# Retention with its state on VectorE, scaled k on ScalarE, later loads of v and an early stretch of zero products

## The chip, the cores and the metric

The kernel runs on one core of one Trainium2 chip. The metric is the device time of one execution in microseconds (us); each run of a kernel gives one such time, and the median counts. Five engines work side by side, each in the order of its own queue, and wait for one another through semaphores: TensorE (PE; PEld is its weight load) multiplies matrices into PSUM, VectorE (DVE) and ScalarE (ACT) work element by element on SBUF and PSUM, GpSimd (POOL) sets up constants, SyncE (SP) issues the loads and stores. Times of a trace are counted from the first instruction; the span ends with the last.

## The reference

Three stages follow each other: a retention (attention with a decaying state, 2 x 8 heads, 768 positions of 64 channels), a feed-forward layer with mish, and one with elu (1536 tokens, 512 to 2048 and back). The feed-forward weights come as 64-bit floats, everything else as 32-bit.

```python
for b in range(nb):                       # blocks of 64 positions
    qb, kb, vb = (q[:, :, sl], k[:, :, sl], v[:, :, sl])
    intra = np.einsum('bhic,bhjc->bhij', qb, kb) * Dmask[None]
    intra = np.einsum('bhij,bhjd->bhid', intra, vb)
    inter = np.einsum('bhid,bhde->bhie', qb * lam_pow[None], kv_state)
    out[:, :, sl] = intra + inter
    kb_dec = kb * rev_pow[None]
    kv_state = lam_block[None, :, None, None] * kv_state + np.einsum('bhsd,bhse->bhde', kb_dec, vb)
...
h = x @ w_in;  g = h * np.tanh(softplus(h));  x = g @ w_out
h = x @ w_in2; g = np.where(h > 0, h, np.exp(h) - 1);  out = g @ w_out2
```

## The kernel before

**Retention** (`retention`, L125) goes through 12 chunks of 128 positions, the two batches in turn; a chunk holds all 8 heads. Iteration n of the loop at L305 writes: the loads of chunk n+3 (`load`), perhaps a load of feed-forward weights (`beside_load`, table `LOAD`), the transposes of k and q of chunk n+1 (`transposes`, L211, copied out of PSUM by ScalarE as kT and qT, L215), the scores of chunk n (`scores`, L240), their product with the decay (`decay`, am, L247, VectorE), k and q of chunk n+1 scaled by powers of lam (`scaled`, kd at L223 and q2 at L230, both VectorE), and the outputs of chunk n-1 (`outputs`): the products o (L269) of the state with q2 and of v with am; xh, ScalarE's rounded copy of o (L274); the new state st (L289), which for a chunk with a state before it is eight products of the diagonal matrix dg (lam to the power 128) with the old state sbd and eight of kd with v, summed in PSUM; ScalarE's copy of st to sbd in two halves (L295), which the outputs of the batch's next chunk read; and xl, the rest o - xh, on VectorE (L296). The outputs' PSUM tile o has one buffer, so the next chunk's outputs wait for xh and xl.

**The weights.** A feed-forward weight tile is loaded as raw 64-bit words by SyncE (`w_load`) into one of four buffers and turned by eight VectorE steps and one ScalarE copy (`w_steps`, L94 to L118) into a high and a low 32-bit half. During retention `beside_step` puts one such step at a time between the retention's own VectorE instructions, from iteration 4 on; the steps of later tiles are spread over the feed-forward units by the tables `FIRST`, `SECOND` and `LATER`.

**Feed-forward.** A unit "in" is 12 products of 128x512 into h (three for each of four blocks of 128 channels: high by high, high by low, low by high), then the activation; a unit "out" is 12 products into y, added to acc on VectorE (L405).

**What sets the order.** A scheduler arranges the instructions of each engine by its own estimate; those given to `pin` keep the order in which they are written. Pinned are the loads, TensorE's retention products, the VectorE operations of the retention and the steps beside them. ScalarE's copies and the feed-forward products are not.

Of the kernel before, what the change touches and what calls it, by code (L numbers as in the profile page):

```python
# [8 lines left out]
F32 = mybir.dt.float32  # L9
# [9 lines left out]
def kernel(  # L19
# [12 lines left out]
    nc = tc.nc  # L32
# [53 lines left out]
    def w_steps(n):  # L86
# [27 lines left out]
        w_load(n + AHEAD)  # L114
# [10 lines left out]
    def retention(beside_load, beside_step, at_end):  # L125
# [12 lines left out]
        def pin(ins):  # L138
            tc.keep_in_program_order(ins)

        def load(n, parts=1):
            if n >= NC:
                return
            b, c = chunks[n]
            for nm, src in (("k", k), ("q", q), ("v", v)):
                t = io.tile([P, H, D], F32, tag=nm + "n", name=nm + "n")
                np_ = 1 if nm == "v" else parts
                for y in range(np_):
                    hs = slice(y * H // np_, (y + 1) * H // np_)
                    pin(nc.sync.dma_start(  # L150
                        out=t[:, hs],
                        in_=src[b, hs, c * P:(c + 1) * P, :].rearrange("h p d -> p h d"),
                    ))
                nat[n, nm] = t

        lam_b = cst.tile([P, H, 1], F32, name="lam_b")
        load(0, 2)
        nc.scalar.dma_start(out=lam_b.rearrange("p h o -> p (h o)"), in_=lam.partition_broadcast(P))
        for n in (1, 2):
            load(n)  # L160
# [27 lines left out]
        while m < P:  # L188
# [5 lines left out]

        dg = cst.tile([P, PR, P], F32, name="dg")
        nc.vector.tensor_tensor(
            out=dg, in0=ident.unsqueeze(1).to_broadcast([P, PR, P]),
            in1=lq[:, :, P - 1:P].to_broadcast([P, PR, P]), op=ALU.mult,
        )
# [4 lines left out]
        def transposes(n):  # L204
            b, c = chunks[n]
            out = []
            for nm in ("k", "q"):
# [7 lines left out]
                nc.scalar.activation(out=t, in_=ps, func=AF.Copy)  # L215
                out.append(t)
            tr[n] = out
        def scaled(n):
            c = chunks[n][1]
            q2 = kd = None  # L220
            if c < NCH - 1:
                kd = wk.tile([P, H, D], F32, tag="kd", name="kd", bufs=3)
                pin(nc.vector.tensor_tensor(  # L223
                    out=kd, in0=nat[n, "k"], in1=dm[:, :, P - 1:P].to_broadcast([P, H, D]),
                    op=ALU.mult,
                ))
                beside_step(n - 1, pin)
# [6 lines left out]
        def scores(n):  # L234
            kT, qT = tr[n]
            ps = psS.tile([P, 2, PR, P], F32, tag="sc", name="sc")
            for r in range(PR):
                for hh in range(2):
                    rows = slice(hh * D, (hh + 1) * D)
                    pin(nc.tensor.matmul(  # L240
                        ps[:, hh, r], lhsT=kT[rows, r], rhs=qT[rows, r], start=True, stop=True
                    ))
            sc[n] = ps

# [7 lines left out]
        def outputs(n):  # L252
# [21 lines left out]
            nc.scalar.activation(out=xh[t][:, :, col:col + P], in_=o, func=AF.Copy)  # L274
            if c < NCH - 1:

                st = psO.tile([P, PR, D], F32, tag="st", name="st")
                terms = []
                if c > 0:
                    terms += [  # L280
                        (r, hh, dg[:, r, hh * D:(hh + 1) * D], sbd[b][:, r, hh * D:(hh + 1) * D])
                        for r in range(PR) for hh in range(2)
                    ]
                terms += [
                    (r, hh, kd[:, 2 * r + hh], vn[:, 2 * r + hh])
                    for r in range(PR) for hh in range(2)
                ]
                for x, (r, hh, lt, rt) in enumerate(terms):
                    pin(nc.tensor.matmul(  # L289
                        st[hh * D:(hh + 1) * D, r], lhsT=lt, rhs=rt,  # L290
                        start=x < 2, stop=x >= len(terms) - 2, skip_group_check=True,
                    ))
                for hh in range(2):
                    rows = slice(hh * D, (hh + 1) * D)
                    nc.scalar.activation(out=sbd[b][rows, :, rows], in_=st[rows], func=AF.Copy)  # L295
# [5 lines left out]
            ))  # L301

        transposes(0)
        scaled(0)
        for n in range(NC + 1):  # L305
            load(n + 3)
# [4 lines left out]
            elif n < NC:  # L311
                if n + 1 < NC:
                    transposes(n + 1)
                scores(n)
# [7 lines left out]
            beside_step(n, pin)  # L322
        at_end()
# [130 lines left out]
    LOAD = {1: 0, 2: 1, 4: 2, 5: 3}  # L454
# [11 lines left out]
    def beside_step(n, pin):  # L466
        if n >= 4:
# [55 lines left out]
```

## Time and profile before

| | us |
|---|---|
| median of 3 runs (595.68 to 596.53) | 595.98 |
| the profiled execution | 595.6 |
| its span, first to last instruction | 593.8 |

A row of the profile's list of groups names the line, the engine, the operation, output and input tiles, the shape, the count, the busy time and the mean length of one. The chain of waits goes back from the last instruction: at each step to what released it, or to the instruction ahead of it on its engine; read in order of time, each piece has a start, a length, an engine and a line. A timeline row has a start, the time from its first start to its last end, the instruction, how many were merged, and in brackets for how long the engine was idle ahead of it and what ended that. A product of 32-bit floats stands as two records (x16 are eight products); a transpose stands as one.

### The profile page before, as it was taken

Reading aid. Unit: us, or ns where it says so; the run is one execution under the profiler, and the core shown is the slowest. Engines: PE = TensorE matmul, PEld = TensorE weight load, DVE = VectorE, ACT = ScalarE, POOL = GpSimd, SP = SyncE. Lnnn points to the kernel's source line nnn. Section 1 sums busy time; section 2 is a strip of 40 time slices with the busy share of each in tenths; the row PEclk is TensorE's granted clock in tenths of the full one; section 3 lists DMA queues with packets and bytes.
Section 4 is the critical chain, followed back from the end, with each engine's and each line's share of the span. In section 5 each row is a group of like instructions: output and inputs, shape, how many; then the busy total and the mean of one; then the engine's idle time right before and its main releaser. Section 6 shows DMA issues by size and latency. Waiting matters only on the chain.

```text
span 593.8 us, 8100 instructions
## 1 busy us (share of the span) xinstructions
PE 583.8 (98%) x3244; PEld 486.2 (82%) x3244; DVE 446.5 (75%) x822; ACT 217.2 (37%) x375; POOL 3.6 (1%) x10
## 2 busy tenths in 40 slices
PE   6999999999999999999999999999999999999997
PEld 4988888888888888888888888888888888888886
DVE  5798798999669943996489985999399966953342
ACT  3454445322242331341245453253254334244230
POOL 2000000000000000000000000000000000000000
PEclk9999999999999999999999999999999999999999
DMA  9999224224203220232013120233013210000112
GB/s 188 234 233 200 66 78 142 71 74 132 79 18 109 87 72 0 72 124 90 0 40 100 49 96 1 71 108 95 12 40 102 74 68 0 2 0 1 71 53 89
DMA packets 61029, 46.65 MB, mean 79 GB/s; under 512 B 38849, under 2 KB 55489, under 8 KB 60993
## 3 DMA queue, kind: packets, MB, share of 16 engines
q1 hardware_dynamic: 60848, 46.14, 27.6%
q8 instruction: 25, 0.41, 0.3%
q14 instruction: 12, 0.09, 0.0%
q10 hardware_dynamic: 144, 0.00, 0.0%
HBM read 43.00 MB, written 3.15 MB: 78 GB/s over the span
## 4 chain that ended last, share of the span: by engine, by line
PE 98%; DMA 1%; ACT 0%; issue 0%; DVE 0%; ACTq 0%
PE h L351 44%; PE y L393 44%; PE o L269 4%; PE sc L240 2%; PE st L289 1%; PE qTp L211 1%; PE kTp L211 1%; DMA kn<-in_k_dram 1%; ACT sbd L295 0%; ACT qT L215 0%; DVE acc L405 0%; ACTq L295 0%
## 5 line engine op out<-in xcount | busy, mean ns | idle before, releaser
L351 PE MATMUL h<-xh,w 128*128 128x512 f32 x768 | 241.2, 390 | 0.0
L351 PEld LDWEIGHTS h<-xh,w 128*128 128x128 f32 x768 | 143.9, 188 | 30.3 <-issue 0.3
L351 PE MATMUL h<-xl,w 128*128 128x512 f32 x384 | 149.4, 389 | 0.0
L393 PE MATMUL y<-g,w 128*128 128x512 f32 x576 | 133.0, 389 | 0.0
L393 PE MATMUL y<-w,g 128*128 128x512 f32 (+1 forms) x588 | 132.5, 385 | 0.0
L393 PEld LDWEIGHTS y<-w,g 128*128 128x128 f32 x588 | 108.9, 188 | 22.1
L393 PEld LDWEIGHTS y<-g,w 128*128 128x128 f32 x576 | 108.1, 188 | 22.5
L405 DVE TENSOR_TENSOR acc<-acc,y 128x512 f32<-128x512 f32 (+1 forms) x73 | 49.4, 677 | 57.7 <-PE y L393 57.6
L117 ACT ACTIVATE w<-m 128x512 fp32r<-128x512 f32 x64 | 40.2, 629 | 135.3 <-DVE m L115 71.9
L361 DVE TENSOR_TENSOR g<-g,g 128x512 fp32r<-128x512 f32 x96 | 65.7, 686 | 26.6 <-ACT g L360 26.3
L351 PEld LDWEIGHTS h<-xl,w 128*128 128x128 f32 x384 | 72.1, 188 | 15.0
L360 ACT ACTIVATE g<-g 128x512 fp32r<-128x512 f32 x96 | 59.8, 629 | 16.5 <-DVE g L378 15.4
L118 DVE TENSOR_TENSOR w<-m,w 128x512 fp32r<-128x512 f32 x64 | 43.7, 686 | 19.3 <-ACT w L117 18.6
L369 ACT ACTIVATE g<-h 128x512 f32<-128x512 f32 x48 | 28.1, 597 | 71.8 <-PE h L351 71.8
L375 ACT ACTIVATE e<-h 128x512 f32<-128x512 f32 x48 | 28.6, 596 | 65.7 <-PE h L351 65.0
L111 DVE SCALAR_TENSOR_TENSOR u<-raw,u 128x512 f32<-128x512 uint32 x64 | 43.6, 683 | 0.1
L104 DVE SCALAR_TENSOR_TENSOR b<-raw,b 128x512 int32<-128x512 int32 x64 | 43.6, 683 | 0.1
L115 DVE TENSOR_TENSOR m<-b,u 128x512 f32<-128x512 f32 x64 | 43.5, 683 | 0.1
L378 DVE SCALAR_TENSOR_TENSOR g<-e,h 128x512 f32<-128x512 f32 x48 | 32.7, 682 | 13.2 <-ACT e L376 13.2
L376 ACT ACTIVATE e<-e 128x512 f32<-128x512 f32 x48 | 30.2, 630 | 1.0
L107 DVE TENSOR_SCALAR u<-b 128x512 int32<-128x512 int32 x64 | 26.6, 420 | 0.3
L94 DVE TENSOR_SCALAR m<-raw 128x512 int32<-128x512 int32 x64 | 26.6, 420 | 0.3
(45 smaller groups left out, 288.2 us busy)
## 6 DMA issues: line engine op xcount, KB each, us to landing
raw<-in_moe_w_in_dram SPq DMA_DIRECT2D x32, 512.0 KB, 3.7
raw<-in_moe_w_out_dram SPq DMA_DIRECT2D x32, 512.0 KB, 3.3
vn<-in_v_dram SPq DMA_DIRECT2D x12, 256.0 KB, 5.1
kn<-in_k_dram SPq DMA_DIRECT2D x11, 256.0 KB, 5.1
qn<-in_q_dram SPq DMA_DIRECT2D x11, 256.0 KB, 5.2
out_dram<-acc SPq DMA_DIRECT2D x11, 256.0 KB, 2.0
kn<-in_k_dram SPq DMA_DIRECT2D x2, 128.0 KB, 3.3
qn<-in_q_dram SPq DMA_DIRECT2D x2, 128.0 KB, 3.4
```

The lines of the kernel that those rows point to most:

```text
L104: yield nc.vector.scalar_tensor_tensor(out=b, in0=hw, scalar=-0x40000000, in1=b, op0=ALU.bitwise_and, op1=ALU.bitwise_or)
L111: yield nc.vector.scalar_tensor_tensor(out=uf, in0=lw, scalar=2.0 ** -52, in1=uf, op0=ALU.mult, op1=ALU.mult)
L115: yield nc.vector.tensor_tensor(out=mf, in0=bf, in1=uf, op=ALU.add)
L117: nc.scalar.activation(out=w[:, 0], in_=mf, func=AF.Copy)
L118: yield nc.vector.tensor_tensor(out=w[:, 1], in0=mf, in1=w[:, 0].bitcast(F32), op=ALU.subtract)
L351: nc.tensor.matmul(h, lhsT=lt, rhs=rt, start=(kk == 0 and n == 0), stop=(kk == KD - 1 and n == 2),)
L360: nc.scalar.activation(out=gg[:, 0], in_=g, func=AF.Copy)
L361: nc.vector.tensor_tensor(out=gg[:, 1], in0=g, in1=gg[:, 0].bitcast(F32), op=ALU.subtract)
L376: nc.scalar.activation(out=e, in_=e, func=AF.Exp, scale=-1.0)
L378: nc.vector.scalar_tensor_tensor(out=g, in0=e, scalar=-1.0, in1=h, op0=ALU.add, op1=ALU.max)
L393: nc.tensor.matmul(y, lhsT=lt, rhs=rt, start=(i == 0 and n == 0), stop=(i == G - 1 and n == 2),)
L405: nc.vector.tensor_tensor(out=dst, in0=dst, in1=y, op=ALU.add)
```

## The change

- The state is kept in a tile sd for each batch. VectorE multiplies it by lam to the power 128 (after the products of st are issued) and, after xl and one weight step, adds st, which now holds kd and v alone; a batch's first state is copied. ScalarE copies sd, not st, to sbd. The eight products with dg and dg itself are gone.
- kd is made by ScalarE, eight pieces of 128x64, each scaled by a column of dm, in place of one VectorE multiplication.
- v of a chunk is loaded after k and q of the next one, and in the loop one iteration later than these.
- Eleven products of a tile of zeros are written at the beginning (`warm`): seven ahead of the transposes of chunk 0, four behind them.
- All of ScalarE's retention work is pinned. The weights' loads of tiles 4 to 7 are issued at iterations 9 to 12 and not by a step; the steps start at iteration 3 and stand at three places of an iteration, not four. The first two feed-forward units are issued after the last scores.

```diff
@@ -111,7 +111,8 @@
         yield nc.vector.scalar_tensor_tensor(
             out=uf, in0=lw, scalar=2.0 ** -52, in1=uf, op0=ALU.mult, op1=ALU.mult
         )
-        w_load(n + AHEAD)
+        if n >= PG - AHEAD:
+            w_load(n + AHEAD)
         yield nc.vector.tensor_tensor(out=mf, in0=bf, in1=uf, op=ALU.add)
         w = wp.tile([P, 2, DM], F32R, tag=f"w{side}", name=f"w{side}", bufs=(6, 8)[side])
         nc.scalar.activation(out=w[:, 0], in_=mf, func=AF.Copy)
@@ -137,16 +138,17 @@
 
         def pin(ins):
             tc.keep_in_program_order(ins)
-
-        def load(n, parts=1):
-            if n >= NC:
+            return ins
+
+        def load(n, names, parts=1):
+            if not 0 <= n < NC:
                 return
             b, c = chunks[n]
-            for nm, src in (("k", k), ("q", q), ("v", v)):
+            for nm in names:
+                src = {"k": k, "q": q, "v": v}[nm]
                 t = io.tile([P, H, D], F32, tag=nm + "n", name=nm + "n")
-                np_ = 1 if nm == "v" else parts
-                for y in range(np_):
-                    hs = slice(y * H // np_, (y + 1) * H // np_)
+                for y in range(parts):
+                    hs = slice(y * H // parts, (y + 1) * H // parts)
                     pin(nc.sync.dma_start(
                         out=t[:, hs],
                         in_=src[b, hs, c * P:(c + 1) * P, :].rearrange("h p d -> p h d"),
@@ -154,10 +156,11 @@
                 nat[n, nm] = t
 
         lam_b = cst.tile([P, H, 1], F32, name="lam_b")
-        load(0, 2)
+        load(0, "kq", 2)
         nc.scalar.dma_start(out=lam_b.rearrange("p h o -> p (h o)"), in_=lam.partition_broadcast(P))
         for n in (1, 2):
-            load(n)
+            load(n, "kq")
+            load(n - 1, "v")
 
         ident = cst.tile([P, P], F32, name="ident")
         make_identity(nc, ident)
@@ -191,12 +194,8 @@
                 in1=lq[:, :, m - 1:m].to_broadcast([P, PR, m]), op=ALU.mult,
             )
             m *= 2
-
-        dg = cst.tile([P, PR, P], F32, name="dg")
-        nc.vector.tensor_tensor(
-            out=dg, in0=ident.unsqueeze(1).to_broadcast([P, PR, P]),
-            in1=lq[:, :, P - 1:P].to_broadcast([P, PR, P]), op=ALU.mult,
-        )
+        lc = lq[:, :, P - 1:P].to_broadcast([P, PR, D])
+        sd = [cst.tile([P, PR, D], F32, name=f"sd{b}") for b in range(B)]
         sbd = [cst.tile([P, PR, P], F32, name=f"sbd{b}") for b in range(B)]
         for t in sbd:
             nc.gpsimd.memset(t, 0.0)
@@ -212,7 +211,7 @@
                         ps[:, r], x[:, 2 * r:2 * r + 2].rearrange("p h d -> p (h d)"), ident
                     ))
                 t = wk.tile([P, PR, P], F32, tag=nm + "T", name=nm + "T")
-                nc.scalar.activation(out=t, in_=ps, func=AF.Copy)
+                pin(nc.scalar.activation(out=t, in_=ps, func=AF.Copy))
                 out.append(t)
             tr[n] = out
         def scaled(n):
@@ -220,11 +219,11 @@
             q2 = kd = None
             if c < NCH - 1:
                 kd = wk.tile([P, H, D], F32, tag="kd", name="kd", bufs=3)
-                pin(nc.vector.tensor_tensor(
-                    out=kd, in0=nat[n, "k"], in1=dm[:, :, P - 1:P].to_broadcast([P, H, D]),
-                    op=ALU.mult,
-                ))
-                beside_step(n - 1, pin)
+                for x in range(H):
+                    pin(nc.scalar.activation(
+                        out=kd[:, x], in_=nat[n, "k"][:, x], func=AF.Copy,
+                        scale=dm[:, x, P - 1:P],
+                    ))
             if c > 0:
                 q2 = wk.tile([P, PR, P], F32, tag="q2", name="q2", bufs=3)
                 pin(nc.vector.tensor_tensor(out=q2, in0=tr[n][1], in1=lq, op=ALU.mult))
@@ -237,10 +236,11 @@
             for r in range(PR):
                 for hh in range(2):
                     rows = slice(hh * D, (hh + 1) * D)
-                    pin(nc.tensor.matmul(
+                    last = pin(nc.tensor.matmul(
                         ps[:, hh, r], lhsT=kT[rows, r], rhs=qT[rows, r], start=True, stop=True
                     ))
             sc[n] = ps
+            return last
 
         def decay(n):
             a = wk.tile([P, 2, PR, P], F32, tag="am", name="am")
@@ -271,39 +271,51 @@
                     start=x < 2, stop=x >= len(terms) - 2, skip_group_check=True,
                 ))
             t, col = divmod(n * P, TB)
-            nc.scalar.activation(out=xh[t][:, :, col:col + P], in_=o, func=AF.Copy)
+            pin(nc.scalar.activation(out=xh[t][:, :, col:col + P], in_=o, func=AF.Copy))
             if c < NCH - 1:
-
                 st = psO.tile([P, PR, D], F32, tag="st", name="st")
-                terms = []
+                for x in range(H):
+                    r, hh = divmod(x, 2)
+                    pin(nc.tensor.matmul(
+                        st[hh * D:(hh + 1) * D, r], lhsT=kd[:, x], rhs=vn[:, x],
+                        start=True, stop=True,
+                    ))
                 if c > 0:
-                    terms += [
-                        (r, hh, dg[:, r, hh * D:(hh + 1) * D], sbd[b][:, r, hh * D:(hh + 1) * D])
-                        for r in range(PR) for hh in range(2)
-                    ]
-                terms += [
-                    (r, hh, kd[:, 2 * r + hh], vn[:, 2 * r + hh])
-                    for r in range(PR) for hh in range(2)
-                ]
-                for x, (r, hh, lt, rt) in enumerate(terms):
-                    pin(nc.tensor.matmul(
-                        st[hh * D:(hh + 1) * D, r], lhsT=lt, rhs=rt,
-                        start=x < 2, stop=x >= len(terms) - 2, skip_group_check=True,
-                    ))
-                for hh in range(2):
-                    rows = slice(hh * D, (hh + 1) * D)
-                    nc.scalar.activation(out=sbd[b][rows, :, rows], in_=st[rows], func=AF.Copy)
+                    pin(nc.vector.tensor_tensor(out=sd[b], in0=sd[b], in1=lc, op=ALU.mult))
             pin(nc.vector.tensor_tensor(
                 out=xl[t][:, :, col:col + P],
                 in0=o,
                 in1=xh[t][:, :, col:col + P].bitcast(F32),
                 op=ALU.subtract,
             ))
-
+            beside_step(n + 1, pin)
+            if c < NCH - 1:
+                if c > 0:
+                    pin(nc.vector.tensor_tensor(out=sd[b], in0=sd[b], in1=st, op=ALU.add))
+                else:
+                    pin(nc.vector.tensor_copy(sd[b], st))
+                for hh in range(2):
+                    rows = slice(hh * D, (hh + 1) * D)
+                    pin(nc.scalar.activation(
+                        out=sbd[b][rows, :, rows], in_=sd[b][rows], func=AF.Copy
+                    ))
+
+
+        idle = cst.tile([P, P], F32, name="idle")
+        nc.vector.memset(idle, 0.0)
+
+        def warm(count):
+            ps = psO.tile([P, PR, P], F32, tag="o", name="warm")
+            for _ in range(count):
+                pin(nc.tensor.matmul(ps[:, 0], lhsT=idle, rhs=idle, start=True, stop=True))
+
+        warm(7)
         transposes(0)
+        warm(4)
         scaled(0)
         for n in range(NC + 1):
-            load(n + 3)
+            load(n + 3, "kq")
+            load(n + 2, "v")
             beside_load(n, pin)
             if n == 0:
                 scores(0)
@@ -311,7 +323,7 @@
             elif n < NC:
                 if n + 1 < NC:
                     transposes(n + 1)
-                scores(n)
+                last = scores(n)
             if n < NC:
                 decay(n)
             beside_step(n, pin)
@@ -319,8 +331,8 @@
                 scaled(n + 1)
             if n > 0:
                 outputs(n - 1)
-            beside_step(n, pin)
-        at_end()
+        with tc.issue_after(last.ins):
+            at_end()
         es.close()
 
 
@@ -451,7 +463,7 @@
         g, i = divmod(n, PG)
         u = (FIRST, SECOND)[g][i] if g < 2 else LATER[i] + (g - 2) * 24
         at.setdefault(u, []).append(n)
-    LOAD = {1: 0, 2: 1, 4: 2, 5: 3}
+    LOAD = {1: 0, 3: 1, 5: 2, 7: 3, 9: 4, 10: 5, 11: 6, 12: 7}
 
     def beside():
         for n in range(BESIDE):
@@ -464,7 +476,7 @@
             pin(w_load(LOAD[n]))
 
     def beside_step(n, pin):
-        if n >= 4:
+        if n >= 3:
             ins = next(todo, None)
             if ins is not None:
                 pin(ins)
```

**ScalarE, middle of the retention stage.** Names: kT, qT copies of the transposes; xh the copy of the outputs; sbd the state that TensorE reads; sd the state on VectorE; kd pieces of scaled k. Before, one chunk, with a weight copy w in it:

```order
L295 ACTIVATE sbd_143<-st 64x4x64 x2
L215 ACTIVATE kT<-kTp 128x512
L117 ACTIVATE w_549<-m 128x512
L215 ACTIVATE qT<-qTp 128x512
L274 ACTIVATE xh_65<-o 128x4x128
L295 ACTIVATE sbd_144<-st 64x4x64 x2
```

Now, one chunk, at the one place where five pieces of the next chunk stand ahead of sbd:

```order
L214 ACTIVATE kT<-kTp 128x512
L214 ACTIVATE qT<-qTp 128x512
L223 ACTIVATE kd<-kn,dm 128x64 x8
L274 ACTIVATE xh_65<-o 128x4x128
L118 ACTIVATE w_785<-m 128x512
L223 ACTIVATE kd<-kn,dm 128x64 x5
L299 ACTIVATE sbd_141<-sd_139 64x4x64 x2
```

Eight pieces of kd stand between qT and xh of every chunk, and sbd reads sd, which VectorE writes, in place of st.

**VectorE, the same place.** am is the decayed scores, q_... the scaled q, xl the rest of the outputs; m, b, u are steps of a weight tile. Before, one chunk's turn:

```order
L247 TENSOR_TENSOR am<-sc,dm 128x1024
L107 TENSOR_SCALAR u<-b 128x512
L223 TENSOR_TENSOR kd<-kn,dm 128x512
L111 SCALAR_TENSOR_TENSOR u<-raw,u 128x512
L230 TENSOR_TENSOR q_506<-qT,lq 128x512
L115 TENSOR_TENSOR m<-b,u 128x512
L296 TENSOR_TENSOR xl_68<-o,xh_65 128x4x128
L118 TENSOR_TENSOR w_549<-m,w_549 128x512
```

Now:

```order
L247 TENSOR_TENSOR am<-sc,dm 128x1024
L104 SCALAR_TENSOR_TENSOR b<-raw,b 128x512
L229 TENSOR_TENSOR q_478<-qT,lq 128x512
L107 TENSOR_SCALAR u<-b 128x512
L284 TENSOR_TENSOR sd_140<-sd_140,lq 128x256
L285 TENSOR_TENSOR xl_67<-o,xh_64 128x4x128
L111 SCALAR_TENSOR_TENSOR u<-raw,u 128x512
L294 TENSOR_TENSOR sd_140<-sd_140,st 128x256
```

The addition of st to sd stands behind xl and a weight step; kd has left the queue.

**TensorE, first feed-forward products.** Before, h stands between scores and outputs of retention chunks from chunk 7 on:

```order
L240 MATMUL sc<-qT,kT 128x128 x8
L351 MATMUL h<-xh_64,w_549 128x512 x2
L351 MATMUL h<-xl_67,w_549 128x512
L269 MATMUL o<-q_590,sbd_144 64x128 x8
L269 MATMUL o<-am,vn 64x128 x8
L289 MATMUL st<-sbd_144,dg 64x64 x8
L289 MATMUL st<-vn,kd 64x64 x8
```

Now the first h stands behind the last scores:

```order
L239 MATMUL sc<-qT,kT 128x128 x8
L269 MATMUL o<-q_797,sbd_142 64x128 x8
L269 MATMUL o<-am,vn 64x128 x8
L279 MATMUL st<-vn,kd 64x64 x8
L239 MATMUL sc<-qT,kT 128x128 x8
L363 MATMUL h<-xh_64,w_559 128x512
L363 MATMUL h<-xl_67,w_559 128x512
```

The products with dg are gone, and no feed-forward product is left inside the retention stage ahead of the last scores.

## Rows read from the trace of the kernel before

**Rows 1.** The page, part 1: busy time, share of the span, instructions of each engine.

```profile
PE 583.8 (98%) x3244; PEld 486.2 (82%) x3244; DVE 446.5 (75%) x822; ACT 217.2 (37%) x375; POOL 3.6 (1%) x10
```

**Rows 2.** The chain of waits in order of time: start, length, what.

```profile
4.11 1.15 PE kTp L211 x4
...
17.43 0.59 PE kTp L211 x4
...
31.03 0.39 ACT sbd L295
...
31.43 0.39 ACT sbd L295
...
43.54 0.67 PE h L351 x2
...
50.02 0.89 PE h L351 x3
...
55.86 1.90 PE o L269 x32
57.75 0.93 PE st L289 x32
...
59.27 0.44 PE qTp L211 x4
...
63.63 1.09 PE sc L240 x16
...
155.11 10.88 PE y L393 x48
```

**Rows 3.** The timeline of ScalarE: start, length, instruction, idle time ahead of it.

```profile
52.86 0.60 ACT L274 ACTIVATE xh<-o 128x512 fp32r<-128x512 f32 x1 [2.85 <-PE o L269]
...
54.66 0.60 ACT L215 ACTIVATE kT<-kTp 128x512 f32<-128x512 f32 x1
55.15 0.59 ACT L215 ACTIVATE qT<-qTp 128x512 f32<-128x512 f32 x1
```

**Rows 4.** The timeline of VectorE, with one row of ScalarE (72.47).

```profile
29.29 0.42 DVE L94 TENSOR_SCALAR m<-raw 128x512 int32<-128x512 int32 x1
29.62 0.68 DVE L223 TENSOR_TENSOR kd<-kn,dm 128x512 f32<-128x512 f32 x1
...
31.49 0.68 DVE L296 TENSOR_TENSOR xl<-o,xh 128x512 fp32r<-128x512 f32 x1
32.09 0.68 DVE L104 SCALAR_TENSOR_TENSOR b<-raw,b 128x512 int32<-128x512 int32 x1
...
71.74 0.69 DVE L115 TENSOR_TENSOR m<-b,u 128x512 f32<-128x512 f32 x1
72.47 0.63 ACT L117 ACTIVATE w<-m 128x512 fp32r<-128x512 f32 x1 [0.44 <-DVE m L115]
...
589.06 0.42 DVE L405 TENSOR_TENSOR acc<-acc,y 128x256 f32<-128x256 f32 x1 [0.74 <-PE y L393]
```

**Rows 5.** Lines L295, L215 (ns min/median/max); last the page's group of L117.

```profile
L295 ACT ACTIVATE sbd<-st x20: 377/378/381, 17.5 to 64.1; 64x256 f32<-64x256 f32 x20
L215 ACT ACTIVATE kT<-kTp x12: 597/597/598, 5.3 to 59.6; 128x512 f32<-128x512 f32 x12
L117 ACT ACTIVATE w<-m 128x512 fp32r<-128x512 f32 x64 | 40.2, 629 | 135.3 <-DVE m L115 71.9
```

**Rows 6.** The timeline of the beginning, VectorE and TensorE.

```profile
5.46 2.28 DVE L174 TENSOR_TENSOR_SCAN dm<-step,eye 128x1024 f32<-128x1024 f32 x1
7.13 2.08 PE L240 MATMUL sc<-qT,kT 64*128 64x128 f32 x16 [0.69 <-ACT qT L215]
```

**Rows 7.** Stretches: length, busy time of PE, PEld, DVE, ACT, POOL, PEclk, DMA share, GB/s.

```profile
10.00:15.00 5.00, 4.16 (x22) 3.09 (x22) 1.93 (x3) 2.39 (x4) 0.00 (x0) 1.00 1.29 216
```

**Rows 8.** VectorE's timeline (first out-weight's last step); the chain's first out-products.

```profile
73.13 0.69 DVE L118 TENSOR_TENSOR w<-m,w 128x512 fp32r<-128x512 f32 x1 [0.70 <-ACT w L117]
...
84.39 2.72 PE y L393 x12
```

## The prediction

> **What bounds the kernel now.** The page first: TensorE is busy 98% of the span, VectorE 75%, ScalarE 37% [rows 1]. The chain of waits, in order of time, then says which stretch is worth looking at. From 63.63 us, where the scores of chunk 11 start, it names TensorE alone to the last product, one of 512 columns after another, 48 of them in 10.88 us, so 0.227 us each [rows 2]. There the time is a count of products, and the change takes none away and adds none. Whatever it gains or costs is therefore read at one point: **when do the scores of chunk 11 start**, and how many feed-forward products are done by then. Before, that is 63.63 us, with five done in gaps of the retention stage (two at 43.54, three at 50.02) [rows 2]. In the changed order the first feed-forward product stands behind those scores: five products come back behind the point, 5 x 0.227 = 1.13 us.
>
> Up to 63.63 a chunk's round on TensorE is 0.59 + 0.44 (transposes of k and q) + 1.09 (scores) + 1.90 (outputs) + 0.93 (state) = 4.95 us [rows 2]. ScalarE stands idle for 2.85 us before an xh copy [rows 3]: a stage bound by TensorE, with room on ScalarE and hardly a wait that lies on the end.
>
> **The state on VectorE** takes the eight products with dg from each of the eight chunks that have a state before and after, half of the 32 records of 0.93 us [rows 2]: 8 x 0.47 = 3.8 us less on TensorE, and a round of 4.48. That is a gain only where TensorE stays what ends the round.
>
> **The new round of ScalarE.** In the order, ScalarE now does for every chunk: copy of kT, copy of qT, eight scaled pieces kd, xh of two chunks earlier, two copies sbd. All are in one queue, and the last two wait for a chain that was not there: xh, then on VectorE xl, a step of the weights, and the addition to sd (the program's order puts the step between), then sbd. Before, sbd was read from TensorE's result alone. Queued behind the waiting sbd is the kT copy of the next chunk but one, and everything behind that; TensorE's outputs wait for xl, which waits for xh. So ScalarE's work and this wait add up to one round, from one xh to the next:
>
> xh 0.60 [rows 3]; 0.04 at the handover, as between VectorE's m and ScalarE's w, and 0.60 from xl's start to the next VectorE operation [rows 4]; the step, 0.33 from start to start for a one-operand one, 0.60 for a two-operand one [rows 4]; the addition of 128x256 out of PSUM, 0.42 like the accumulation of that size [rows 4]; 0.04 again; two sbd copies at 0.40 from start to start [rows 2], and 0.03 more each for a source in SBUF (629 against 597 ns [rows 5]); kT and qT, 0.49 from start to start and 0.50 for the second [rows 3]. Together 0.60 + 0.04 + 0.60 + 0.33 + 0.42 + 0.04 + 0.86 + 0.99 = 3.88 us with a light step, 4.15 with a heavy one, 3.55 with none, and eight pieces kd on top. With any price of a piece over 0.08 us this is more than TensorE's 4.48.
>
> **The price of a piece, k.** No row shows an activation of 128x64. From both sides: the line through 378 ns for 64x256 and 597 for 128x512 [rows 5] gives 0.214 for 64 elements, 0.246 from SBUF. If a piece overlaps with the next as kT does with qT (0.60 long, 0.49 apart [rows 3]), k is 0.15, the low end. The smallest distance that the trace shows between two activations is 0.40, the sbd pair [rows 2]: the high end. I take k = 0.26, its own length and 0.01 between, because the short copies of the trace (0.39 long, 0.40 apart) show no overlap.
>
> The Trainium skill ("ScalarE: Activation LUTs", section "What ACT_TABLE_LOAD costs") gives an activation 186 ns and 0.833 ns an element, 93 more for a scale that is a pointer, and lets neighbours overlap by 93: for 64 elements an estimate of 0.24 us, and by it the sum below would be 598.0. The trace agrees on 512 elements (613 by the page, 597 and 629 here) and on the overlap of kT and qT, and differs on the sbd pair, which doesn't overlap.
>
> **The sum.** The scan that makes dm ends at 5.46 + 2.28 = 7.74 us [rows 6], and nothing of the change moves it; the first kd waits for it, and all of ScalarE behind that. Three groups of kd and two pairs kT, qT later, xh of chunk 0 starts at 7.78 + 2.00 + 24k. Then the rounds by the order: two without a step (7.10), chunk 2 to 3 light (3.88), 3 to 4 heavy with a weight copy of 0.52 in it (4.67; 0.63 less the overlap), 4 to 5 light (3.88), 5 to 6 heavy (4.15), 6 to 7 with a weight copy and five pieces inside the wait (0.60 + 0.04 + 0.60 + 0.68 + 0.04 + 0.52 + 0.86 + 0.99 = 4.33), 7 to 8 light and without kd (3.88), and 3.98 to the end of the last qT: 35.87, with seven groups of kd. The scores of chunk 11 start at 7.78 + 2.00 + 35.87 + 80k = **45.65 + 80k**. With k = 0.26 that is 66.45, 2.8 us later than before; with the 1.13 of the five products the change costs 3.9 us. The profiled execution took 595.6 (span 593.8), the median of the runs is 0.4 higher: 599.5 on the profiled one's terms, **599.9** on the median's. The point of no change is 45.65 + 80k + 1.13 = 63.63, k = 0.21.
>
> **The other edits, taken at nothing.** *v one chunk later*: the loads bring 216 GB/s at the beginning [rows 7], 256 KB in 1.2 us, so k and q of chunk 2 land some 1.2 us earlier, but ScalarE is then at the pieces of chunk 1 (until 9.8 + 1.0 + 8k = 12.9), which covers it; without that delay it would be worth the 1.2 us. *Products of zeros*: seven ahead of the first k, which lands at 4.11 [rows 2], where TensorE is idle, and four ahead of the first scores. The first transposes took 1.15 us, those at 17.43 0.59 [rows 2], as at TensorE's levels of 1.2 and 2.4 GHz, although the window from 10 to 15 us gives a granted clock of 1.00 [rows 7]. If the zeros bring the fast rate forward, what falls away lies where ScalarE waits for dm; if not, the four cost 1.0 to 2.1 us (half the 2.08 of eight paired scores, or all of it [rows 6]), of which up to 1.6 would reach the kT copy of chunk 1 and so the end. *kd off VectorE, sd on it*: 10 x 0.68 against 18 x 0.42 [rows 4], within 1 us on an engine that waits in this stage. *The weights' loads and steps*: the first out-product starts at 84.39 and its weight was ready at 73.82 [rows 8]; that slack of 10 us covers 3 to 5 us of delay, and is gone only if retention's end moves by more.
>
> **Rivals.** (1) *Short pieces overlap on ScalarE; not slower.* kT and qT do so; the sbd pair does not, and a scale from memory can only add. At k = 0.15 the beginning is then held by the loads: the seventh, q of chunk 2, lands at about 4.6 + 6 x 1.2 = 11.9, and with its transposes, scores and outputs of chunk 0 the first xh starts at 14.5. Then 14.5 + 35.87 + 56 x 0.15 = 58.8, and 595.6 - 4.8 + 1.1 = 591.9, 592.3 on the median. It decides below k = 0.21. (2) *ScalarE's wait is not what ends the round*, because sbd's successors get by or VectorE is earlier than the order lets it: TensorE and the loads set it, 4.48 a round, scores of chunk 11 at 55 to 57, so 588 to 590. Against it: the order shows one queue, with sbd ahead of kT. (3) *Dear pieces*, k = 0.33 to 0.40: the read of the scale comes on top and nothing overlaps: 72.1 to 77.7, so 605 to 611. (4) *TensorE falls to its lower level* in the gaps that the longer rounds leave it (6.0 against 4.48, 1.5 us in each). A round at that level is 8.96 of products, 3 us over mine; three such rounds give 609. The trace shows no gap of that length at the high level, for or against.
>
> **How the numbers follow.** My case (k of 0.22 to 0.32, 597 to 605) 52%; k of 0.20 to 0.22, no change, 8%; rival 1 21%; rival 2 4%; rival 3 11%; rival 4 4%. About 0.2% is what a measurement of this kernel can tell from no change. Faster 0.25, same 0.08, slower 0.67. The range goes from 590.5, under rival 1's 592.3, to 607 (k = 0.35): rival 2, the upper part of 3 and most of 4 lie outside, some 15%.
>
> **What would show it.** In the profile after: kd pieces of 0.25 to 0.35 us, 0.26 apart; ScalarE from 8 to 60 us either busy or waiting for the sd addition; xh starts 5.6 to 6.3 us apart; TensorE idle some 1.5 us a round, waiting for VectorE's xl ahead of the outputs; scores of chunk 11 at 66; from there no gap. Wrong it would be with k under 0.21, with xh starts 4.5 us apart, or with a TensorE that waits for weights behind 70 us.

## The result, and the profile after

The changed kernel takes **601.8 us** (median of five runs, 600.93 to 601.83) against 595.98 of the kernel before: a ratio of 1.0092, 95% interval 1.0078 to 1.0105. It is slower by 0.8 to 1.05%, within the forecast range and 1.9 us over its number. The profiled execution took 601.83 us with a span of 600.0; before, these were 595.6 and 593.8.

The page's part 1 and the engines of its chain of waits, of the kernel after:

```profile
PE 583.4 (97%) x3138; PEld 486.7 (81%) x3138; DVE 446.0 (74%) x830; ACT 236.2 (39%) x455; POOL 3.6 (1%) x10
...
PE 89%; ACT 5%; DVE 2%; DMA 2%; SPq 1%; issue 1%; ACTq 0%
```

Beside [rows 1] only ScalarE's busy time moved by more than 1 us, from 217.2 to 236.2 us. What is new is in the chain: ScalarE has 5% of it, and its largest line there is kd. The chain also names two loads of q (2%). The first, which ends at 11.79 us, holds up TensorE ahead of the first xh. The second ends at 37.86, but the piece that it is said to release starts 0.62 us after qT (37.26 to 37.88), as in the other rounds, so it isn't shown to hold anything up. The timeline of TensorE after, around the point at which the prediction reads everything:

```profile
68.40 1.16 PE L239 MATMUL sc<-qT,kT 64*128 64x128 f32 x16 [0.29 <-ACT qT L214]
69.50 0.50 PE L363 MATMUL h<-xh,w 128*128 128x512 f32 x1
```

The scores of chunk 11 start at 68.40 us, not 63.63 [rows 2], and the first feed-forward product stands behind them. So 4.8 us of the 6.2 us by which the span grew is a later end of the retention stage. From these scores to the last addition on VectorE it takes 1.2 us more than before (68.40 to 596.46, against 63.63 to 590.50), where the five products that no longer fit into gaps are 1.1 us. The last 0.2 us lies behind that addition. From 69.50 on TensorE runs without a gap that matters, as before.

A round of ScalarE after, from its timeline (start, length, instruction, idle time ahead of it), with a light weight step in it:

```profile
27.59 0.58 ACT L274 ACTIVATE xh<-o 128x512 fp32r<-128x512 f32 x1
29.65 0.85 ACT L299 ACTIVATE sbd<-sd 64x256 f32<-64x256 f32 x2 [1.48 <-DVE sd L294]
30.53 0.60 ACT L214 ACTIVATE kT<-kTp 128x512 f32<-128x512 f32 x1
31.02 0.59 ACT L214 ACTIVATE qT<-qTp 128x512 f32<-128x512 f32 x1
31.64 2.02 ACT L223 ACTIVATE kd<-kn,dm 128x64 f32<-128x64 f32 x8
33.57 0.57 ACT L274 ACTIVATE xh<-o 128x512 fp32r<-128x512 f32 x1
```

It is the round the prediction wrote down: xh, a wait of 1.48 us for VectorE's addition, two sbd, kT, qT, eight pieces, xh. Where ScalarE idled 2.85 us before an xh [rows 3], it now goes from the last piece into xh without idling, and idles behind xh instead. The waits after from 0 to 70 us (who, for whom, us in total, times, longest) show the ring:

```profile
ACT sbd L299 <- DVE sd L294: 10.9, 6, 2.5
PE o L269 <- DVE xl L285: 8.1, 7, 2.5
DVE xl L285 <- ACT xh L274: 6.7, 6, 1.8
```

ScalarE waits for VectorE's sum, VectorE's xl for ScalarE's xh, TensorE's outputs for xl: three engines wait for each other in one loop.

### The profile page after: what moved, and what is told of

Read it like the earlier page. It is cut to its first block, busy times and chain, and to the rows that moved or that the text cites. A ratio compares the mean times of both kernels' runs of the same rounds, so it can differ in the third digit from the quotient of the medians.

```text
span 600.0 us, 7979 instructions
## 1 busy us (share of the span) xinstructions
PE 583.4 (97%) x3138; PEld 486.7 (81%) x3138; DVE 446.0 (74%) x830; ACT 236.2 (39%) x455; POOL 3.6 (1%) x10
## 4 chain that ended last, share of the span: by engine, by line
PE 89%; ACT 5%; DVE 2%; DMA 2%; SPq 1%; issue 1%; ACTq 0%
PE h L363 44%; PE y L405 44%; ACT kd L223 2%; DMA qn<-in_q_dram 2%; PE o L269 1%; SPq L152 1%; ACT sbd L299 1%; ACT kT L214 1%; ACT qT L214 1%; PE sc L239 1%; ACT xh L274 0%; DVE sd L294 0%; DVE q L229 0%; DVE b L104 0%; DVE xl L285 0%
## 5 line engine op out<-in xcount | busy, mean ns | idle before, releaser
L100 DVE TENSOR_SCALAR b<-m 128x512 int32<-128x512 int32 x64 | 26.8, 421 | 0.3
```

## What the experiments tell apart

**Theory A** is the prediction's: ScalarE's one queue sets the round, since the eight pieces stand between qT and xh, and the wait for VectorE's addition behind xh has nothing in it. **Rival B**: eight pieces are too dear on ScalarE wherever they stand, or the state on VectorE is. **Rival C**: something else sets the rounds, the loads or TensorE's lower clock level. Ratios are to the kernel before, run on the same chip; its medians there lay between 595.57 and 595.77 us.

### The pieces of k behind xh

Same pieces, same engine, another place in its queue (`pieces(n)` holds the eight activations that stood in `scaled(n)`):

```diff
-                for x in range(H):
-                    pin(nc.scalar.activation(
-                        out=kd[:, x], in_=nat[n, "k"][:, x], func=AF.Copy,
-                        scale=dm[:, x, P - 1:P],
-                    ))
+            if n < 2:
+                kds[n] = pieces(n)
...
             pin(nc.scalar.activation(out=xh[t][:, :, col:col + P], in_=o, func=AF.Copy))
+            kds[n + 2] = pieces(n + 2)
```

> The eight kd pieces stand behind xh instead of ahead of it in ScalarE's queue (from chunk 2 on), nothing else changes. Theory A (ScalarE's queue: the pieces and the wait for xl, step and addition add up to one round): the pieces of 1.9 us now run inside the wait of 1.5 to 1.8, the round falls from some 6.0 us to about 4.5 to 4.7 (0.60 + 1.93 + 0.86 + 0.99 and handovers), the scores of chunk 11 start at 57 to 58, 590 to 592 us. Theory B (the pieces are too dear on ScalarE wherever they stand): ScalarE's work is the same, so no change, 601 to 602. Theory C (loads or TensorE's lower level make the longer rounds): no change or under 2 us.

Measured: **592.84 us, ratio 0.9950 (0.9935 to 0.9965)**; scores of chunk 11 at 58.71. Both are 0.7 to 0.8 us over the stretches expected by theory A; the time is 8 us under the one expected by B. The timeline of ScalarE:

```profile
18.85 0.60 ACT L282 ACTIVATE xh<-o 128x512 fp32r<-128x512 f32 x1
19.48 2.02 ACT L224 ACTIVATE kd<-kn,dm 128x64 f32<-128x64 f32 x8
21.41 0.84 ACT L308 ACTIVATE sbd<-sd 64x256 f32<-64x256 f32 x2
22.27 0.60 ACT L214 ACTIVATE kT<-kTp 128x512 f32<-128x512 f32 x1
22.76 0.59 ACT L214 ACTIVATE qT<-qTp 128x512 f32<-128x512 f32 x1
23.40 0.60 ACT L282 ACTIVATE xh<-o 128x512 fp32r<-128x512 f32 x1
```

And its waits from 0 to 70 us:

```profile
ACT sbd L308 <- DVE sd L303: 4.6, 5, 2.5
...
PE qTp L210 <- DMA qn<-in_q_dram: 2.6, 6, 0.6
```

The same work in a round of 4.55 us: the pieces now fill the time in which VectorE makes xl and the sum, and sbd follows them at once. The wait for the sum falls from 10.9 to 4.6 us. Moving eight instructions takes 9 us off and turns a loss of 0.9% into a gain of 0.5%. That is theory A, and against B. Behind it the loads begin to show (qTp waits for q in six rounds).

### The pieces as one multiplication on VectorE again

```diff
-                for x in range(H):
-                    pin(nc.scalar.activation(
-                        out=kd[:, x], in_=nat[n, "k"][:, x], func=AF.Copy,
-                        scale=dm[:, x, P - 1:P],
-                    ))
+                pin(nc.vector.tensor_tensor(
+                    out=kd, in0=nat[n, "k"], in1=dm[:, :, P - 1:P].to_broadcast([P, H, D]),
+                    op=ALU.mult,
+                ))
```

> kd goes back to VectorE as one multiplication; state, v, zeros and ScalarE's order stay as changed. Theory A: ScalarE's round is 3.9 to 4.2 us without the pieces and no longer ends the round; VectorE has 1.13 + 0.60 + 0.60 + three steps of 0.46 + 0.35 + 0.60 + 0.35 = 5.0 us a chunk and is the next bound; scores of chunk 11 at 61 to 63, 594 to 596. Theory C (loads, lower level): 600 to 602, since neither is touched.

Measured: **593.24 us, ratio 0.9957 (0.9940 to 0.9974)**, scores of chunk 11 at 59.96. It is 0.8 us under the expected stretch, and the next limit is in the windows (stretch, length, busy time of PE, PEld, DVE, ACT, POOL, granted clock, DMA share, GB/s):

```profile
30.00:40.00 10.00, 9.27 (x147) 8.35 (x146) 9.98 (x19) 5.13 (x11) 0.00 (x0) 1.00 1.10 226
40.00:50.00 10.00, 9.05 (x144) 7.98 (x143) 9.97 (x18) 4.96 (x11) 0.00 (x0) 1.00 0.97 218
```

VectorE works 9.98 of 10 us: kd and the state together fill it. The loop is gone all the same, since ScalarE, with 5.1 us of work in 10, has time for the wait. Moving kd to ScalarE makes room on VectorE, but no gain from that room is shown: the medians are 592.84 and 593.24, and the intervals overlap.

### The state's product on TensorE again

The dg products come back, sbd is read from PSUM; the pieces stay on ScalarE ahead of xh.

```diff
+                if c > 0:
+                    terms += [
+                        (r, hh, dg[:, r, hh * D:(hh + 1) * D], sbd[b][:, r, hh * D:(hh + 1) * D])
+                        for r in range(PR) for hh in range(2)
+                    ]
...
+                    pin(nc.scalar.activation(out=sbd[b][rows, :, rows], in_=st[rows], func=AF.Copy))
...
-                    pin(nc.vector.tensor_tensor(out=sd[b], in0=sd[b], in1=st, op=ALU.add))
...
-                        out=sbd[b][rows, :, rows], in_=sd[b][rows], func=AF.Copy
```

> The state goes back to TensorE (products with dg, sbd copied from PSUM); kd stays in pieces on ScalarE, v, zeros and the pinned order stay. Theory A: no wait for VectorE is left between xh and the next kT; ScalarE has 0.6 + 0.8 + 1.1 + 2.0 = 4.5 us a chunk, TensorE 4.95 and is the bound again; scores of chunk 11 at 61 to 63, 594 to 596. Theory B (pieces too dear): rounds stay near 6, 600 to 602.

Measured: **593.21 us, ratio 0.9959 (0.9944 to 0.9974)**, scores of chunk 11 at 59.52. The window in the middle:

```profile
30.00:40.00 10.00, 10.00 (x178) 9.11 (x177) 7.93 (x13) 9.06 (x28) 0.00 (x0) 1.00 0.98 226
```

This too is 0.8 us under the expected stretch. With eight pieces ahead of xh, but without the wait for VectorE, TensorE is busy all the time. So neither the pieces nor the sum alone make the kernel slower than it was: **it takes both**, the pieces ahead of xh and the sum behind it. Each of these three kernels takes one of the two out, and all three stand between 592.8 and 593.3 us. Two kernels were not run: one with neither of the two, and one in which the order of ScalarE's work is not pinned. So what the pinned order costs or saves by itself is not shown.

### The addition ahead of the weight step

```diff
-            beside_step(n + 1, pin)
             if c < NCH - 1:
                 if c > 0:
                     pin(nc.vector.tensor_tensor(out=sd[b], in0=sd[b], in1=st, op=ALU.add))
                 else:
                     pin(nc.vector.tensor_copy(sd[b], st))
+            beside_step(n + 1, pin)
+            if c < NCH - 1:
...
```

> The addition of st to sd stands ahead of the weight step on VectorE, behind xl; nothing else changes. Theory A: the step (0.33 or 0.60 us) leaves the wait of sbd in some seven rounds, 2.5 to 3.5 us in all: 598 to 599.5. Theory B and C: the step is not on the path, 601 to 602.

Measured: **598.85 us, ratio 1.0050 (1.0035 to 1.0065)**, scores of chunk 11 at 65.50. ScalarE's timeline: rounds with pieces of 5.64 to 6.15 us, and the wait that is left without a step in it:

```profile
33.08 0.57 ACT L274 ACTIVATE xh<-o 128x512 fp32r<-128x512 f32 x1
34.80 0.85 ACT L300 ACTIVATE sbd<-sd 64x256 f32<-64x256 f32 x2 [1.15 <-DVE sd L293]
```

One instruction of VectorE in another place lets the scores of chunk 11 start 2.90 us earlier: what VectorE does between xh and the sum is on the path, as the prediction's sum has it.

### Four more pieces a chunk

The slope of the sum, 80k, tested from above: four more copies behind each chunk's eight.

```diff
+                more = wk.tile([P, H, D], F32, tag="more", name="more", bufs=2)
+                for x in range(H // 2):
+                    pin(nc.scalar.activation(
+                        out=more[:, x], in_=nat[n, "k"][:, x], func=AF.Copy,
+                        scale=dm[:, x, P - 1:P],
+                    ))
```

> The changed kernel with four more scaled copies of 128x64 behind each chunk's eight, into a tile that nobody reads (the result stays as it is, the time of ScalarE does not). The pieces stood 0.241 us apart in the changed kernel. Theory A (all pieces of all ten chunks lie in the round that sets the end, as in the prediction's 80k): 10 x 4 x 0.241 = 9.6 us more, 610 to 612. Rival B' (a good part of the pieces hides beside the wait for VectorE's addition): at most half of it, 603 to 606.5.

Measured: **610.51 us, ratio 1.0250 (1.0236 to 1.0264)**, scores of chunk 11 at 77.08, 8.68 us later. ScalarE's timeline shows one round as it grew from 5.98 to 6.93 us:

```profile
31.49 0.58 ACT L280 ACTIVATE xh<-o 128x512 fp32r<-128x512 f32 x1
33.55 0.85 ACT L305 ACTIVATE sbd<-sd 64x256 f32<-64x256 f32 x2 [1.48 <-DVE sd L300]
```

The wait behind xh is the same 1.48 us: the pieces don't hide in it. Seven rounds with pieces grew by 0.94 to 0.96 us each, 6.7 in all (4 x 0.241 is 0.96). Ahead of the first xh, where three groups stand, only 2.0 of 2.9 us came through, since there ScalarE had idled 0.77 us for the outputs of chunk 0. So nine of the ten groups count (8.68 / 0.96), not ten.

### v loaded early again

In the changed kernel, and in the one with the pieces behind xh:

```diff
-        load(n + 2, "v")
+        load(n + 3, "v")
```

(and likewise at the beginning, v of chunk 0 ahead of k of chunk 1).

> The changed kernel with v loaded in the same round as k and q again, as before. The prediction took the later v at nothing, since ScalarE would cover the later k and q. In the kernel with the pieces behind xh the same edit cost 1.8 us. If the prediction's cover holds: 601.6 to 602.3. If k and q of chunk 2, later by one v (1.2 us), delay the first outputs and no later round makes it up: 602.6 to 603.4.

> As the kernel with the pieces behind xh (592.84), but v is loaded in the same round as k and q again, three chunks ahead, and v of chunk 0 ahead of k of chunk 1. One v took some 1.2 us on SP's queue, so k and q of chunks 1 and 2 land 1 to 1.2 us later each. Theory A (ScalarE binds; a late load is made up by idle time within two rounds): 592.6 to 593.4. Rival C (loads bind once ScalarE's pieces are out of the way): 593.8 to 594.8.

Measured: **602.97 us, 1.0124 (1.0111 to 1.0138)**, scores of chunk 11 0.94 us later than in the changed kernel; and **594.65 us, 0.9983 (0.9975 to 0.9992)** against 0.9950 with v late. So the later v is worth about 1 us in the changed kernel (span 601.0 against 600.0) and 2 us where the pieces are out of the way. TensorE's timeline of the first of the two:

```profile
11.77 0.63 PE L211 MATMUL kTp<-ident,kn 128*128 128x128 f32 x4 [1.76 <-DMA kn<-in_k_dram]
12.98 1.08 PE L211 MATMUL qTp<-ident,qn 128*128 128x128 f32 x4 [0.58 <-DMA qn<-in_q_dram]
```

In the changed kernel these two start at 10.73 and 11.92 us: one v later, k and q of chunk 2 land 1.05 us earlier, and the first xh follows (16.30 against 17.21).

### Without the products of zeros

```diff
-        idle = cst.tile([P, P], F32, name="idle")
-        nc.vector.memset(idle, 0.0)
...
-        warm(7)
         transposes(0)
-        warm(4)
```

> The changed kernel without the products of zeros. The prediction took them at nothing. The trace of the changed kernel had TensorE at the half rate again at 12.5 us, behind gaps of 1.57 and 0.56 us, so the zeros had given away most of what they brought: 601.5 to 602.3. If what is left of it (kTp and qTp of chunk 0 at the fast rate) reaches the scores of chunk 11: 602.3 to 603.

> As the kernel with the pieces behind xh (592.84), without the products of zeros at the beginning. If the fast rate of TensorE comes as late as in the kernel before (first scores 2.08 us instead of 1.16 at some 7 us) and the beginning reaches through to the scores of chunk 11: plus 0.5 to 1.0, 593.3 to 593.9. If the loads set when the second and third chunk can start: 592.6 to 593.1.

Measured: **602.02 us, 1.0104 (1.0091 to 1.0118)**, and **591.91 us, 0.9935 (0.9923 to 0.9947)** against 0.9950 with zeros: no difference beyond the intervals in either. The first is in the stretch for zeros that have given away what they brought; the second is 0.7 us under both of its stretches. The two timelines of TensorE tell why. With zeros (the changed kernel):

```profile
8.57 0.60 PE L210 MATMUL qTp<-ident,qn 128*128 128x128 f32 x4
10.73 0.63 PE L210 MATMUL kTp<-ident,kn 128*128 128x128 f32 x4 [1.57 <-DMA kn<-in_k_dram]
11.92 0.63 PE L210 MATMUL qTp<-ident,qn 128*128 128x128 f32 x4 [0.56 <-DMA qn<-in_q_dram]
12.48 2.08 PE L239 MATMUL sc<-qT,kT 64*128 64x128 f32 x16
14.49 1.76 PE L269 MATMUL o<-am,vn 128*64 128x128 f32 x16
```

Its window of 10 to 15 us, with the granted clock behind POOL's column:

```profile
10.00:15.00 5.00, 3.71 (x30) 3.13 (x32) 0.40 (x2) 5.00 (x19) 0.00 (x0) 0.75 1.35 218
```

Without zeros, the timeline and then the same window:

```profile
9.11 1.11 PE L210 MATMUL kTp<-ident,kn 128*128 128x128 f32 x4
10.02 1.06 PE L210 MATMUL qTp<-ident,qn 128*128 128x128 f32 x4
10.91 1.12 PE L210 MATMUL kTp<-ident,kn 128*128 128x128 f32 x4
11.82 1.06 PE L210 MATMUL qTp<-ident,qn 128*128 128x128 f32 x4
12.81 1.44 PE L239 MATMUL sc<-qT,kT 64*128 64x128 f32 x16
14.18 1.09 PE L269 MATMUL o<-am,vn 128*64 128x128 f32 x16
```

```profile
10.00:15.00 5.00, 5.00 (x46) 4.18 (x45) 1.15 (x2) 4.49 (x15) 0.00 (x0) 1.00 1.32 218
```

The zeros do bring the fast rate forward, to some 6 us. The faster TensorE then runs out of work, waits 1.57 and 0.56 us for k and q of chunk 2, and does the next scores at half rate. Without zeros it works at half rate up to 12 us, from 7.10 on with no gap, and is fast from the outputs of chunk 0 on (1.09 us against 1.76). Both reach the first xh at 16.3 to 16.4 us, the one by the loads and a slow end, the other by a slow beginning: in the changed kernel the zeros only choose which products are slow. In the trace with the pieces behind xh, TensorE with zeros stayed fast through these gaps, and the first xh stands at 14.61 us against 15.14 without them; but the scores of chunk 11 start at 58.71 and 58.76, so there too nothing of it reaches the end.

### The cures together

Pieces behind xh and the addition ahead of the step, with and without zeros (both edits stand above):

> The changed kernel with both cures at once: the eight pieces of k stand behind xh (of the chunk two later), and the addition to the state stands ahead of the weight step that follows xl. Theory A (the round on ScalarE is still what bounds the chunks): with the pieces behind xh ScalarE still waited 4.6 us in all for the addition (10 to 70 us); the addition ahead of the step takes two thirds of that away, so 592.84 less 1.5 to 3, 590 to 591.5. Rival C (with the pieces behind xh the loads of k and q bound: qTp waited 2.6 us for them, kTp 1.0): what ScalarE saves is waited for at the loads, 592.3 to 593.3.

> Pieces behind xh, addition ahead of the weight step, and no products of zeros. In the kernel with the first two the first xh stood at 16.39 us, in the one without zeros at 15.14, since TensorE then stays busy from 5 to 15 us at the fast rate. Rounds of 4.2 to 4.4 us from there: scores of chunk 11 up to 1.2 us earlier than 58.69, so 590.6 to 591.8. Rival C (loads of q set the rounds by then): no gain, 591.7 to 592.2.

Measured: **591.81 us, 0.9934 (0.9921 to 0.9947)**, and **591.30 us, 0.9931 (0.9917 to 0.9945)**, with scores of chunk 11 at 58.69 and 57.76. The last is 0.7% faster than the kernel before and 1.7% faster than the changed one. The intervals of these two and of the kernel with late pieces and no zeros overlap, so which is best stays open. The first, 591.81, lies between the stretches of theory A and rival C and decides for neither. With zeros the first xh stands at 16.39 us there, behind scores at half rate, and without them at 15.24; whether the zeros cost something in that order the medians don't show. The addition's place matters less with the pieces behind xh (592.84 to 591.81) than ahead of it (601.80 to 598.85). The reason that the second expectation gives is not what the traces show: without zeros TensorE is busy from 7.3 us on, but at half rate up to some 12 us, and at the fast rate only then.

## Why the prediction was right, and where its sum was off

**The mechanism holds step by step**: one queue on ScalarE, rounds with pieces of 5.63 to 6.75 us where 5.6 to 6.3 was forecast, TensorE idle ahead of the outputs for xl (1.33 us at 34.92), no gap behind the scores of chunk 11. That the sum came within 1.9 us is in part luck: two errors of opposite sign stood in it, and with k right it would have been 3.4 us too low.

**k was mis-sized, -1.5 us.** The prediction took 0.26 and argued from the sbd pair [rows 2] that short copies don't overlap. Durations of the lines after (ns min, median, max):

```profile
L223 ACT ACTIVATE kd<-kn,dm x80: 331/333/350, 7.8 to 59.1; 128x64 f32<-128x64 f32 x80
...
L299 ACT ACTIVATE sbd<-sd x20: 401/414/418, 18.0 to 72.1; 64x256 f32<-64x256 f32 x20
```

A piece is 0.333 us long, longer than the 0.25 that I gave it, but eight take 2.02, so they stand (2.02 - 0.333) / 7 = 0.241 apart and do overlap. The sbd pair, half the partitions wide, still doesn't (0.44 apart). The row to go by was kT and qT, not the shortest copies. The Trainium skill ("ScalarE: Activation LUTs", section "What ACT_TABLE_LOAD costs") gives for such a piece an estimate of 186 + 64 x 0.833 + 93 = 332 ns, and 93 of overlap between neighbours, so 0.239 us. The trace agrees on both for the pieces among themselves (0.333 and 0.241), but not on the overlap of the sbd pair. The prediction's 598.0 by that price is on the profiled execution's terms, 0.4 more on the median's. Its low end for k, 0.15, is 0.14 by its own rows (0.246 less the 0.11 by which kT and qT overlap), which changes no conclusion. With 0.241 the sum's start is 45.65 + 80 x 0.241 = 64.93, and its time 598.4.

**Four terms were missing, +3.5 us**, from 64.93 to 68.40:

| place | forecast with k = 0.241 | measured | why |
|---|---|---|---|
| first xh | 15.56 | 16.30 | loads, and outputs at half rate (above) |
| rounds 0 to 4 and 5 to 8 (seven) | 39.6 | 40.5 | mostly the first piece, which doesn't overlap with qT |
| round 4 to 5 | 5.81 | 6.43 | xl behind a step that waits for ScalarE |
| last xh of the sum to the scores of chunk 11 | 3.98 | 5.15 | q and a step ahead of xl, no longer covered |

*First xh.* The prediction took it as bound by ScalarE alone and the later v at nothing. In truth ScalarE idled 0.77 us there for the outputs; with twelve pieces it is bound by ScalarE, and the same formula gives 9.78 + 36 x 0.241 = 18.46 against 18.30. *qT to the first piece* takes 0.61 to 0.62 us from start to start in the rounds (31.02 to 31.64), not 0.50. Ahead of the first xh it took 0.48, as these two rows show; why the two differ stays open.

```profile
13.04 0.58 ACT L214 ACTIVATE qT<-qTp 128x512 f32<-128x512 f32 x1
13.52 2.02 ACT L223 ACTIVATE kd<-kn,dm 128x64 f32<-128x64 f32 x8
```

The other two stand in VectorE's timeline after:

```profile
37.89 0.69 DVE L229 TENSOR_TENSOR q<-qT,lq 128x512 f32<-128x512 f32 x1 [0.36 <-ACT qT L214]
40.45 0.69 DVE L119 TENSOR_TENSOR w<-m,w 128x512 fp32r<-128x512 f32 x1 [1.87 <-ACT w L118]
41.06 0.42 DVE L284 TENSOR_TENSOR sd<-sd,lq 128x256 f32<-128x256 f32 x1
41.39 0.68 DVE L285 TENSOR_TENSOR xl<-o,xh 128x512 fp32r<-128x512 f32 x1
...
63.40 0.69 DVE L229 TENSOR_TENSOR q<-qT,lq 128x512 f32<-128x512 f32 x1 [0.62 <-ACT qT L214]
64.01 0.69 DVE L104 SCALAR_TENSOR_TENSOR b<-raw,b 128x512 int32<-128x512 int32 x1
64.61 0.42 DVE L284 TENSOR_TENSOR sd<-sd,lq 128x256 f32<-128x256 f32 x1
64.95 0.68 DVE L285 TENSOR_TENSOR xl<-o,xh 128x512 fp32r<-128x512 f32 x1
```

At 40.45 the step ahead of xl needs the weight copy, which stands behind the eight pieces on ScalarE: xl comes 1.07 us after xh's start (40.32), not 0.64. At 63.40 the work ahead of xl (q, a step, the state's multiplication) is what VectorE did during the pieces in every round before. These chunks have no pieces, xh starts at 63.25, and xl follows 1.70 us later. The prediction counted what stands behind xl, not what stands ahead of it.

**The edits taken at nothing.** *v later*: wrong, worth 1 us here; ScalarE didn't cover it, as above. *Zeros*: right in size. The fast rate came forward, as in the first of the prediction's two cases, but was lost again behind the gaps, which it did not foresee. *kd off VectorE*: right, VectorE's busy time is 446.0 us against 446.5. *Weights*: right; TensorE has no gap for them.

**The rivals.** Rivals 1 and 3 fall with 0.241, above the 0.21 of no change and below the 0.33 of dear pieces. Rival 2 falls: take the wait or the pieces away and 9 us go. Rival 4 is there in small: behind a gap of 2.48 us at 39.65 the second half of the outputs ran at half rate, with a granted clock of 0.82 from 40 to 45 us and 0.84 from 45 to 50. ScalarE set the end of these rounds all the same (6.43 and 6.23 us). The kernel without zeros shows it: it has the same gap, and behind it TensorE stayed fast (granted clock 1.00 from 40 to 50 us), yet its rounds took 6.43 and 6.24 us. First the changed kernel, then the one without zeros:

```profile
42.13 1.09 PE L269 MATMUL o<-q,sbd 128*64 128x128 f32 x16 [2.48 <-DVE xl L285]
43.06 1.77 PE L269 MATMUL o<-am,vn 128*64 128x128 f32 x16
...
42.21 1.09 PE L269 MATMUL o<-q,sbd 128*64 128x128 f32 x16 [2.48 <-DVE xl L285]
43.13 1.04 PE L269 MATMUL o<-am,vn 128*64 128x128 f32 x16
```

At the first xh the half rate did cost something, as the table says. What rival 2 describes, TensorE and the loads setting the rounds, is what the kernels with the pieces behind xh show, at 591 to 593 us and not 588 to 590.

## What to carry to other kernels

When work moves to an engine with idle time, ask *where* in its queue that idle time lies: here 2.85 us lay ahead of xh, but the new wait opened behind it, and the same eight instructions cost 9 us ahead of xh that they did not cost behind it. For every wait that a change puts in, list what stands ahead of the awaited instruction on its own engine, and what used to cover it. A faster start of one engine is worth nothing where loads set its next step, and can be given back in the gap that it opens.

## What was not expected of the hardware

Activations of 128x64 with a scale from memory overlap by 0.09 us with each other (0.333 long, 0.241 apart), while in the rounds of the changed kernel a 128x512 copy out of PSUM and the first such piece behind it don't (0.59 long, 0.61 to 0.62 apart). Ahead of the first xh these two overlap as well (0.58 long, 0.48 apart).

Gaps of TensorE alone don't tell whether its clock falls. After 1.57 and 0.56 us with 0.63 us of products between, it went to the lower level (granted clock 0.75 from 10 to 15 us). After 1.03 and 0.57 us (pieces behind xh), and after one gap of 1.65 us (four more pieces), the next scores took 1.16 us, the fast rate. Gaps of 1.2 to 1.5 us in the rounds of the changed kernel did not lower it. The one of 2.48 us did there, and the same gap in the kernel without zeros did not. With four more pieces gaps of 2.13, 2.32 and 3.43 us did, and one of 2.45 us did not. At the very beginning products run at half rate while the granted clock reads 1.00 (scores of 2.08 us without zeros), so that column says nothing there.
